# Four-tile attention visits in a fused retention and MLP kernel, with a new emission order

## The chip, the cores and the metric

The kernel runs on one core of one Trainium2 chip. The metric is the device time of one execution in microseconds; for the kernel before there are three runs. One more execution was taken by the hardware profiler. In its rows PE is TensorE (matmuls), PEld the weight loads that overlap it, DVE VectorE, ACT ScalarE, POOL GpSimd, SP SyncE. L701 is line 701 of the kernel's file.

## The reference

A causal retention layer without softmax, then an MLP with exact GELU:

```python
scores = scale * np.matmul(q, k.transpose(0, 1, 3, 2))      # q, k, v: (8, 8, 576, 64)
Dmat = np.where(rel >= 0, gamma[:, None, None] ** rel, 0.0) # rel = pos_i - pos_j, gamma by head
attn_out = np.matmul(scores * Dmat, v)
x = attn_out.transpose(0, 2, 1, 3).reshape(4608, 512)
h = x @ w_in                                                # (512, 2048)
g = 0.5 * h * (1.0 + erf(h / sqrt(2)))
out = g @ w_out                                             # (2048, 512)
```

## The kernel before

The retention runs in chunks of 128 positions (four of them and a tail of 64 per sequence). A unit is one chunk of one batch entry, all eight heads; after the first four units two batch entries form a pair (j = 0, 1) and are handled in one visit. For a chunk of a pair the tensor engine does four things:

- scores (`scores`, L535): keys times queries inside the chunk, 32 matmuls of 64x64 weights on 128 columns, into four PSUM banks `sc`. `masked` (L558, VectorE) multiplies them by the causal mask into `ret`.
- inner (`inner`, L600): scaled values `vh` times `ret`, eight matmuls per unit with weights of 128 rows and 64 columns, into one bank `o_ps` per unit.
- state (`state`, L619): keys times `vh`, 16 matmuls per pair with 128 rows and 64 columns, accumulated over chunks in one bank `u_ps`; `either` copies it to `u_sb` on VectorE or ScalarE, whichever the planner has free first.
- cross (`cross`, L653): the state up to the chunk before, times the queries, 16 matmuls of 64x64, added into the `o_ps` banks. `evacuate` (L672) scales them by `dqT` into `xT`, the input of the MLP.

A visit is emitted as inner of the pair that was scored earlier, its state, scores of the next pair, cross; sometimes scores stand alone. The tail chunk has its own forms (L525, L591). `scaled_v` makes `vh`, on VectorE in one instruction or on ScalarE in eight. The first groups are transposed on PE (L482), the later ones by DMA on SP's queue.

The MLP works on blocks of 512 tokens: `mlp1` (L701, `hT`) with GELU on ScalarE, `mlp2` (L746) for the first block, `part` (L885, `m`) with seven products of half blocks in place of eight for the others, `fast` (L966, `f`) in the same manner for the first product of the last blocks. Fillers (`warm`, L1180) run where the planner sees PE idle at the start.

Order is set at build time by a planner. It keeps a clock per engine (`T`), adds a duration for each piece (`pe`, `on`), follows which of the eight PSUM banks are held, and picks the next piece for PE. The string `ORDER` holds the order of loads on POOL's queue (k1, wi0, v5, ...) and numbers that shift the planner's choices by unit: s, b and z delay scores, inner and masks, p and u shift MLP pieces, and a names the units whose values ScalarE scales.

Of the kernel before, what the change touches and what calls it, by code (L numbers as in the profile page):

```python
# [9 lines left out]
FP32 = mybir.dt.float32  # L10
# [7 lines left out]
def kernel(  # L18
# [57 lines left out]
    AHEAD = 14  # L76
    A_TURNS = 2
    HOT = 5.3
    N_WARM = 10
    HOLD = 9  # L80

# [106 lines left out]
    def sum_w(i):  # L188
        w = w_out_sb[i]
        s = w_sum[i] = const.tile([128, 5, 256], BF16, name=f"w_sum{i}")  # L190
        b11, b12, b21, b22 = w[:, 0, 0:256], w[:, 0, 256:512], w[:, 1, 0:256], w[:, 1, 256:512]
        nc.vector.tensor_tensor(s[:, 0], b11, b22, op=ALU.add)
        nc.vector.tensor_tensor(s[:, 1], b12, b22, op=MINUS)
        nc.vector.tensor_tensor(s[:, 2], b21, b11, op=MINUS)
        nc.vector.tensor_tensor(s[:, 3:5], w[:, :, 0:256], w[:, :, 256:512], op=ALU.add)
        ws_at[i] = on("dve", 1.05, land_out[i]) + SEM

    SW_LATE, HW_LATE = 4.2, 2.8
    TURN_SHARES, STORE_SHARES = (0.455, 0.545), (0.455, 0.545)
# [125 lines left out]
    for x, keys in enumerate(zip(*HW_FIRST)):  # L325
        for n, (what, i) in enumerate(keys):
            land[what, i] = (4.6, 5.2)[n] + 0.75 * x
            t = tiles_of(i)
            cast_due[what, i] = (t[1] if what == "v" else t[0][:, "qk".index(what)], first[what, i])
    ORDER = ("wi1 k1 wi0 io q1 v0 q2 k2 v1 wi2 v2 k3 wi3 q3 v3 wi4 wi5 wi6 k4 q5 k5 q4 v5 wi7 wo1 wo0 k6 v4 dq2 "  # L330
# [7 lines left out]
             "b21+6.0").split()  # L338

    BY_ACT = {int(x[1:]) for x in ORDER if x[0] == "a"}  # L340
    S_LATE = {int(x[1:].split("+")[0]): float(x.split("+")[1]) for x in ORDER if x[0] == "s"}
# [106 lines left out]
    def u_of(bp, ci):  # L448
        return u_sb[2 if (bp, ci) == (1, 0) else ci % 2]
# [113 lines left out]
    def scaled_v(i):  # L563
        if len(later) > HP + 1:
            finish_later()
        ci = units[i][1]
        vh = vh_pool.tile([128, H, D], BF16, tag="vh", name="vh")
        at = land["v", i]
        by_act = i in BY_ACT
        if by_act:  # L570
            for h in range(H):
                nc.scalar.activation(vh[:, h, :], loaded[i][1][:, h, :], AF.Copy, scale=dv[:, h, ci:ci + 1])  # L572
            st[i]["V"] = on("act", 2.0, at) + SEM
        else:
            nc.vector.tensor_tensor(vh, loaded[i][1], dv[:, :, ci:ci + 1].to_broadcast([128, H, D]), op=ALU.mult)
            st[i]["V"] = on("dve", 0.685, at) + SEM
        st[i]["vh"] = vh
# [4 lines left out]
    def inner(i):  # L582
        bp, ci, j = units[i]
        s = st[i]
        pe_waits(max(s["R"], s["V"] if "vh" in s and i not in raw else land["v", i]))
        if j is None:
            s["o"] = [bank([128, HP, TAIL], FP32, "o_ps", False) for _ in range(2)]
            for h in range(H):
                for jj in range(2):
                    sl, e = slice(64 * jj, 64 * jj + 64), 64 * (h % 2)  # L590
                    nc.tensor.matmul(s["o"][jj][1][e:e + 64, h // 2, :], lhsT=s["vh"][sl, h, :], rhs=s["ret"][0][sl, h, :],  # L591
                                     start=(h < 2), stop=False, skip_group_check=True)
            s["B"] = pe(0.23, 2 * H, "quad")
        else:
            s["o"] = [bank([128, HP, 128], FP32, "o_ps")]
            o = s["o"][0][1]
            vals = loaded[i][1] if i in raw else s["vh"]
            for hp in range(HP):
                for e in range(2):
                    nc.tensor.matmul(o[64 * e:64 * e + 64, hp, :], lhsT=vals[:, 2 * hp + e, :], rhs=s["ret"][e][:, hp, :],  # L600
                                     start=(hp == 0), stop=(ci == 0 and hp == HP - 1), skip_group_check=True)
            s["B"] = pe(0.23, H, "col")
        s["Bdone"] = True
        if j is None:
            s_done.add(i)
        elif j == 1 and ci < NCI - 1 and (bp, ci) != (1, 0):
            u_due.append((bp, ci))

    def state(bp, ci):
        pair = pair_of[bp, ci]  # L610
        assert (bp, ci) == (1, 0) or nX > (pair_of[bp, ci - 1] if ci else pair_of[bp - 1, NCI - 2] if bp else [-1])[-1]
        if ci == 0:
            u_bank[bp] = bank([128, H, D], FP32, "u_ps")
        u_ps = u_bank[bp][1]
        pe_waits(state_at(bp, ci))
        for h in range(H):
            for j, i in enumerate(pair):
                keys = loaded[i][0][:, 1, h, :] if i < 4 else loaded[i][0][:, 1, h, j, :]
                nc.tensor.matmul(u_ps[64 * j:64 * j + 64, h, :], lhsT=keys, rhs=st[i]["vh"][:, h, :],  # L619
                                 start=(ci == 0 and h == 0), stop=(h == H - 1), skip_group_check=True)  # L620
        done = pe(0.26, 2 * H, "col")
        u_ready[bp, ci] = either(0.68, done, u_of(bp, ci), u_ps) + SEM
        u_due.remove((bp, ci))
        if ci == NCI - 2:
            release(u_bank[bp][0], u_ready[bp, ci])
        for i in pair:
            s_done.add(i)
        if pair[0] >= 4 and next_load[0] < len(groups):
            reload()
# [10 lines left out]
    def cross(n):  # L640
        g = groups[n]
        bp, ci, j0 = units[g[0]]
        if ci == 0:
            return
        u, qT = u_of(bp, ci - 1), sg[n]["qkT"]
        pe_waits(u_ready[bp, ci - 1])
        cols = slice(0, TAIL if j0 is None else C)
        for hp in range(HP):
            for e in range(2):
                for j in range(2):  # L650
                    o = st[g[0]]["o"][j][1] if j0 is None else st[g[j]]["o"][0][1]
                    sl = slice(64 * j, 64 * j + 64)
                    nc.tensor.matmul(o[64 * e:64 * e + 64, hp, :], lhsT=u[sl, 2 * hp + e, :], rhs=qT[sl, 0, 2 * hp + e, cols],  # L653
                                     start=False, stop=(hp == HP - 1), skip_group_check=True)
        done = pe(0.23, 2 * H, "quad")
        for i in g:
            st[i]["B"] = done

# [531 lines left out]
    while True:  # L1190
# [64 lines left out]
        if due:  # L1255
            _, kind, a = due[0]
            if kind == "X":
                cross(group_of[nX])
                for i in groups[group_of[nX]]:
                    evacuate(i)  # L1260
                    nX += 1
            elif kind == "U":
                state(*a)
            elif kind == "S":
                g, back = a
                for i in back:
# [81 lines left out]
```

## Time and profile before

| what | value |
|---|---|
| median of three runs | 285.37 us (285.2 to 285.39) |
| span of the profiled execution | 283.7 us |
| that execution's time outside the span | not given |
| PE busy | 278.0 us, 98%, 3361 matmuls |
| VectorE, ScalarE, GpSimd busy | 70%, 56%, 40% |
| granted TensorE clock | 0.998 |

The span runs from the program's first to its last instruction. A group's mean is the duration of one instruction; matmuls are pipelined, so the next one starts before the last has ended, and the pitch between starts is what a stream of them costs. A wait names who ended an engine's idle time.

### The profile page before, as it was taken

How to read it: one execution, taken by the hardware profiler on the slowest of the kernel's cores; microseconds unless marked ns; L12 is line 12 of the kernel's file. 1: busy time of each engine (PE TensorE's matmuls, PEld its weight loads, DVE VectorE, ACT ScalarE, POOL GpSimd, SP SyncE). 2: the span in 40 equal slices, each digit the busy share in tenths (PEclk: the TensorE clock that was granted, in tenths of full speed). 3: DMA queues.
4: the chain of work that ended last, by engine and by line, in shares of the span. 5: the costliest groups of instructions: out<-in, count | busy, mean ns of one | idle time of the engine just before them, and what ended most of it. 6: DMA issues, size and time to landing. Idle time of an engine off the chain costs nothing.

```text
span 283.7 us, 8075 instructions
## 1 busy us (share of the span) xinstructions
PE 278.0 (98%) x3361; PEld 207.6 (73%) x3361; DVE 199.7 (70%) x412; ACT 158.8 (56%) x362; POOL 114.0 (40%) x143
## 2 busy tenths in 40 slices
PE   8989999999999999999999999999999999999994
PEld 3577666688874588548855778558888888888894
DVE  5753483979865595898178867889669968966822
ACT  5676724755456635693298874564565374665320
POOL 8979987993364465625468552000000000000000
PEclk9999999999999999999999999999999999999999
DMA  9999999999999999999999999910003000400133
GB/s 150 165 182 173 188 180 163 146 142 147 172 161 195 190 147 128 156 229 149 135 197 203 147 137 150 222 21 2 0 2 128 23 2 0 151 0 2 74 114 111
DMA packets 152804, 35.39 MB, mean 125 GB/s; under 512 B 141120, under 2 KB 148928, under 8 KB 152768
## 3 DMA queue, kind: packets, MB, share of 16 engines
q0 software_dynamic: 116832, 18.10, 95.3%
q1 hardware_dynamic: 34528, 16.26, 32.9%
q10 hardware_dynamic: 1408, 0.52, 0.7%
q8 instruction: 26, 0.43, 0.7%
q14 instruction: 10, 0.08, 0.1%
HBM read 36.70 MB, written 9.44 MB: 163 GB/s over the span
## 4 chain that ended last, share of the span: by engine, by line
PE 92%; POOL 3%; DMA 3%; issue 0%; DVE 0%; POOLq 0%
PE m L885 35%; PE hT L701 29%; PE f L966 13%; PE oT L746 5%; PE o_ps L600 3%; PE sc L535 3%; DMA w_in<-in_moe_w_in_dram 3%; POOL qk L318 2%; PE o_ps L653 1%; PE u_ps L619 1%; PE qk_ps L482 1%; POOL v_ld L318 1%; POOL w_in L291 1%; PE sc L525 0%; PE o_ps L591 0%
## 5 line engine op out<-in xcount | busy, mean ns | idle before, releaser
L701 PE MATMUL hT<-xT,w_in 128*128 128x512 bf16 (+3 forms) x560 | 87.4, 312 | 0.8 <-DMA w_in<-in_moe_w_in_dram 0.8
L710 ACT ACTIVATE g<-hT 128x512 bf16<-128x512 f32 (+2 forms) x106 | 57.7, 556 | 36.9 <-PE hT L701 36.1
L701 PEld LDWEIGHTS <-w_in 128*128 128x128 bf16 x560 | 48.4, 98 | 33.8 <-DMA w_in<-in_moe_w_in_dram 1.0
L885 PEld LDWEIGHTS <-gs 128*128 128x128 bf16 x656 | 62.2, 98 | 7.7
L885 PE MATMUL m<-w_sum,gs 128*128 128x256 bf16 (+1 forms) x400 | 47.7, 268 | 0.0
L318 POOL DMA_DIRECT2D v_ld<-in_v_dram x40 | 34.0, 854 | 19.3 <-DMA qk_ld<-in_k_dram 8.8
L318 POOL DMA_DIRECT2D qk_ld<-in_k_dram x36 | 30.4, 851 | 21.7 <-DMA qk_ld<-in_q_dram 19.1
L558 DVE TENSOR_TENSOR ret<-sc,msk 128x512 bf16<-128x512 f32 x48 | 30.2, 683 | 12.2 <-PE sc L535 12.2
L318 POOL DMA_DIRECT2D qk_ld<-in_q_dram x36 | 30.4, 851 | 16.9 <-DMA qkT<-qk_ld 6.5
L885 PE MATMUL m<-w_out,gs 128*128 128x256 bf16 x256 | 32.5, 273 | 0.0
L885 PE MATMUL m<-w_sum,g 128*128 128x256 bf16 x256 | 30.9, 273 | 0.0
L572 ACT ACTIVATE vh<-v_ld,dv 128x64 bf16<-128x64 bf16 x120 | 30.0, 339 | 0.0
L782 DVE TENSOR_TENSOR gs<-g 128x1024 bf16<-128x1024 bf16 x32 | 21.8, 686 | 9.0 <-ACT g L710 8.2
L885 PEld LDWEIGHTS <-g 128*128 128x128 bf16 x256 | 24.9, 98 | 3.9
L991 ACT ACTIVATE g<-f 128x512 bf16<-128x512 f32 x36 | 20.2, 590 | 8.9 <-PE f L966 7.5
L786 DVE TENSOR_TENSOR gs<-g 128x1024 bf16<-128x1024 bf16 x32 | 21.6, 684 | 0.0
L672 DVE TENSOR_TENSOR xT<-o_ps,dqT 128x512 bf16<-128x512 f32 (+1 forms) x32 | 18.4, 617 | 4.5 <-PE o_ps L653 4.4
L966 PEld LDWEIGHTS <-w_in 128*128 128x128 bf16 x192 | 18.8, 98 | 2.2
L461 ACT CAST u_sb<-u_ps 128x512 bf16<-128x512 f32 x15 | 8.7, 587 | 16.0 <-PE u_ps L619 16.0
L461 ACT COPY o<-m 128x512 f32<-128x512 f32 x14 | 8.2, 587 | 15.7 <-PE m L885 15.7
L987 ACT ACTIVATE g<-p 128x512 bf16<-128x512 f32 x12 | 7.6, 630 | 14.1 <-DVE p L985 14.1
L966 PEld LDWEIGHTS <-wi 128*128 128x128 bf16 x144 | 14.0, 98 | 1.6
(96 smaller groups left out, 337.6 us busy)
## 6 DMA issues: line engine op xcount, KB each, us to landing
out_dram<-o SPq DMA_DIRECT2D x27, 256.0 KB, 6.3
v_ld<-in_v_dram POOLq DMA_DIRECT2D x32, 128.0 KB, 9.1
qk_ld<-in_k_dram POOLq DMA_DIRECT2D x28, 128.0 KB, 10.7
qk_ld<-in_q_dram POOLq DMA_DIRECT2D x28, 128.0 KB, 8.6
w_in<-in_moe_w_in_dram POOLq DMA_DIRECT2D x8, 256.0 KB, 7.3
w_out<-in_moe_w_out_dram POOLq DMA_DIRECT2D x8, 256.0 KB, 8.0
out_dram<-o SPq DMA_DIRECT2D x14, 128.0 KB, 2.1
qk_ld<-in_q_dram POOLq DMA_DIRECT2D x8, 64.0 KB, 11.4
```

The costliest lines, as they stand in the source:

```text
L318: nc.gpsimd.dma_start(dst, src[2 * bp + jj, :, ci * C:ci * C + n, :].rearrange("h s d -> s h d"))
L461: nc.scalar.copy(dst, src)
L558: nc.vector.tensor_tensor(r, t, by, op=ALU.mult)
L572: nc.scalar.activation(vh[:, h, :], loaded[i][1][:, h, :], AF.Copy, scale=dv[:, h, ci:ci + 1])
L672: nc.vector.tensor_tensor(x_of(i)[:, :, n * x:n * x + n], o, dqT[:, :, ci * C:ci * C + n], op=ALU.mult)
L701: nc.tensor.matmul(hT[:, m, :], lhsT=w[:, cc, o:o + 128], rhs=x_tiles[t][:, cc, lo:hi], start=(cc == 0), stop=(cc == N_DM - 1))
L710: nc.scalar.activation(g_of(t, m0 // 2)[:, m0 % 2:m0 % 2 + n, lo:hi], hT, AF.Gelu)
L782: nc.vector.tensor_tensor(s.rearrange("p m a b -> p m (a b)"), g[:, :, 0, :], g[:, :, 1, :], op=ALU.add)
L786: nc.vector.tensor_tensor(s, g[:, :, :, LEFT], g[:, :, :, RIGHT], op=MINUS)
L885: nc.tensor.matmul(m[:, 0 if apart else ts, :], lhsT=a, rhs=w[:, c0:c1], start=p in begins and mm == 0 and ts == 0, stop=mm == N_DF // 2 - ...
L966: nc.tensor.matmul(m[:, y, :], lhsT=a[:, c], rhs=d[:, c], start=p in (P1, P7) and y == 0 and c == 0, stop=c == 1, skip_group_check=True)
L991: nc.scalar.activation(g[:, :, rows, cols], m, AF.Gelu)
```

## The change

Output products and state are split along the contraction into halves of 64 rows. Where a pair's inner product, state, scores of the next pair and cross can all run together (`whole`), `visit` emits them as one piece on four 64x64 tiles of the array: three lists of matmuls per tile, woven by their columns. The first part holds inner from a unit's own row half, the state on the diagonal tiles (r == c), cross, and half of the scores on the other tiles. The middle part holds scores alone. The last part holds inner from the other row half, which writes the other unit's bank, the state on the other tiles and the rest of the scores. Ahead of the last part a nop on PE waits for the first matmul of the middle part. The masks, copies and evacuations of the visit follow the whole of it.

The planner's durations are set anew (`BOTH` is that of a visit), and `ORDER` is a new one: its loads are the same up to q4, and behind that loads and all shifts differ.

```diff
+    BOTH = 1.1
-        ws_at[i] = on("dve", 1.05, land_out[i]) + SEM
+        ws_at[i] = on("dve", 1.26, land_out[i]) + SEM
-    ORDER = ("wi1 k1 wi0 io q1 v0 q2 k2 v1 wi2 v2 k3 wi3 q3 v3 wi4 wi5 wi6 k4 q5 k5 q4 v5 wi7 wo1 wo0 k6 v4 dq2 "
-             "wo2 wo3 q7 wo4 k7 dq3 q11 b4+1.0 wo6 v8 wo5 q6 k8 wo7 v6 v7 k9 q10 q9 a28 k11 q8 v11 k10 q12 dq4 v9 "
...
+    ORDER = ("wi1 k1 wi0 io q1 v0 q2 k2 v1 wi2 v2 k3 wi3 q3 v3 wi4 wi5 wi6 k4 q5 k5 q4 wi7 wo0 dq2 v4 wo1 v5 wo2 "
+             "dq3 wo3 k8 wo4 wo7 q6 dq4 k7 wo6 wo5 q7 k6 q8 v6 q9 q11 v10 k9 v8 v7 q10 v12 v9 q12 k10 v11 k11 k12 "
...
-            st[i]["V"] = on("act", 2.0, at) + SEM
+            st[i]["V"] = on("act", 2.7, at) + SEM
-            s["B"] = pe(0.23, 2 * H, "quad")
+            s["B"] = pe(0.15, 2 * H, "quad")
+    HALF = [slice(0, 64), slice(64, 128)]
+
+    def weave(lists):
+        at, last = [0] * len(lists), None
+        while any(lists):
+            x = min((x for x in range(len(lists)) if lists[x]), key=lambda x: at[x])
+            cols, fn, a = lists[x].pop(0)
+            at[x] += cols
+            last = fn(*a)
+        return last
+
+    def whole(g, back):
+        if len(g) != 2 or len(back) != 2 or back[0] < 4 or units[back[0]][2] != 0:
+            return False
...
+        if ci and u_ready.get((bp, ci - 1), 1e9) > T["pe"] + 0.3:
+            return False
...
+        return max(max(st[i].get("V", 1e9), st[i]["R"]) for i in back) <= T["pe"] + 0.3
+
+    def visit(n, bp, ci):
...
+        for i in pair:
+            st[i]["o"] = [bank([128, HP, 128], FP32, "o_ps")]
+        got = [[bank([128, HP, 128], FP32, "sc") for _ in range(2)] for _ in g]
+
+        def inner_mm(j, r, e, hp, first):
+            s = st[pair[j]]
+            vals = loaded[pair[j]][1] if pair[j] in raw else s["vh"]
+            return nc.tensor.matmul(s["o"][0][1][HALF[e], hp, :], lhsT=vals[HALF[r], 2 * hp + e, :],
+                                    rhs=s["ret"][e][HALF[r], hp, :], start=first, stop=(not first and hp == HP - 1),
+                                    skip_group_check=True)
...
+        def state_mm(j, r, h):
+            return nc.tensor.matmul(u_ps[HALF[j], h, :], lhsT=loaded[pair[j]][0][HALF[r], 1, h, j, :],
+                                    rhs=st[pair[j]]["vh"][HALF[r], h, :], start=(ci == 0 and h == 0 and j == r), stop=(h == H - 1),
+                                    skip_group_check=True)
...
+        tiles = [(r, c) for r in range(2) for c in range(2)]
+        parts = [[[] for _ in tiles] for _ in range(3)]
+        for x, (r, c) in enumerate(tiles):
+            one, mid, two = (part[x] for part in parts)
+            one += [(128, inner_mm, (r, r, c, hp, hp == 0)) for hp in range(HP)]
+            two += [(128, inner_mm, (1 - r, r, c, hp, False)) for hp in range(HP)]
+            (one if r == c else two).extend((64, state_mm, (c, r, h)) for h in range(H))
+            if ci:
+                one += [(128, cross_mm, (r, c, hp)) for hp in range(HP)]
+            (two if r == c else one).extend((128, score_mm, (r, c, h)) for h in (range(4, 8) if r == c else range(4)))
+            mid += [(128, score_mm, (r, c, h)) for h in (range(4) if r == c else range(4, 8))]
+        weave(parts[0])
+        _, fn, a = parts[1][0].pop(0)
+        end = fn(*a)
+        weave(parts[1])
+        tc.add_manual_dep(nc.tensor.nop().ins, end.ins.name,
+                          mybir.DependencyInfo(mybir.DependencyClass.Sync, mybir.DependencyReason.DATA), reason="row tiles")
+        weave(parts[2])
+        done = pe(BOTH + (0.23 if ci else 0.0), 12 * H + 2 * H * (ci > 0), "quad")
...
+        u_ready[bp, ci] = either(0.68, done, u_of(bp, ci), u_ps) + SEM
...
+        masked(g[0])
+        for i in pair:
+            evacuate(i)
+        masked(g[1])
-        done = pe(0.26, 2 * H, "col")
+        done = pe(0.24, 2 * H, "col")
-        done = pe(0.23, 2 * H, "quad")
+        done = pe(0.2 if j0 is not None else 0.12, 2 * H, "quad")
                 g, back = a
+                if whole(g, back):
+                    visit(group_of[g[0]], *units[back[0]][:2])
+                    while u_due and state_at(*u_due[0]) <= T["pe"] + 0.3 * (nA >= 8):
+                        state(*u_due[0])
+                    continue
```

More of the change, by code (lines that the diff above doesn't have):

```diff
@@ L329 @@
             cast_due[what, i] = (t[1] if what == "v" else t[0][:, "qk".index(what)], first[what, i])
-    ORDER = ("wi1 k1 wi0 io q1 v0 q2 k2 v1 wi2 v2 k3 wi3 q3 v3 wi4 wi5 wi6 k4 q5 k5 q4 v5 wi7 wo1 wo0 k6 v4 dq2 "
[7 rows of a table removed]
-             "b21+6.0").split()
+    ORDER = ("wi1 k1 wi0 io q1 v0 q2 k2 v1 wi2 v2 k3 wi3 q3 v3 wi4 wi5 wi6 k4 q5 k5 q4 wi7 wo0 dq2 v4 wo1 v5 wo2 "
[7 rows of a table added]
+             "s0+1.0 u7+8 z29+8 p29+29 p24+28 s16+3 u4+28 b1+0.3 s1+0.6 u3+16 u2+8 p26+12").split()
     BY_ACT = {int(x[1:]) for x in ORDER if x[0] == "a"}
@@ L607, in inner @@
             u_due.append((bp, ci))
+    HALF = [slice(0, 64), slice(64, 128)]
[10 more added lines that the diff above has]
+            return False
+        bp, ci, _ = units[back[0]]
+        if (bp, ci) == (1, 0) or back != pair_of.get((bp, ci)) or nX != back[0]:
+            return False
+        if ci and u_ready.get((bp, ci - 1), 1e9) > T["pe"] + 0.3:
+            return False
+        if bp and ci == 1 and nX <= units.index((bp - 1, NCI - 1, None)):
+            return False
+        return max(max(st[i].get("V", 1e9), st[i]["R"]) for i in back) <= T["pe"] + 0.3
@@ new lines, in visit, with cross_mm, score_mm @@
+    def visit(n, bp, ci):
+        pair, g = pair_of[bp, ci], groups[n]
+        if ci == 0:
+            u_bank[bp] = bank([128, H, D], FP32, "u_ps")
+        u_ps, qkT = u_bank[bp][1], sg[n]["qkT"]
+        qT = sg[group_of[pair[0]]]["qkT"]
+        u = u_of(bp, ci - 1) if ci else None
+        at = max(st[i][x] for i in pair for x in "RV")
+        pe_waits(max(at, sg[n]["T"], u_ready[bp, ci - 1] if ci else 0.0))
+        for i in pair:
[7 more added lines that the diff above has]
+                                    skip_group_check=True)
+        def cross_mm(j, e, hp):
+            return nc.tensor.matmul(st[pair[j]]["o"][0][1][HALF[e], hp, :], lhsT=u[HALF[j], 2 * hp + e, :],
+                                    rhs=qT[HALF[j], 0, 2 * hp + e, :], start=False, stop=False, skip_group_check=True)
+        def state_mm(j, r, h):
+            return nc.tensor.matmul(u_ps[HALF[j], h, :], lhsT=loaded[pair[j]][0][HALF[r], 1, h, j, :],
+                                    rhs=st[pair[j]]["vh"][HALF[r], h, :], start=(ci == 0 and h == 0 and j == r), stop=(h == H - 1),
+                                    skip_group_check=True)
+        def score_mm(j, c, h):
+            return nc.tensor.matmul(got[j][h % 2][1][HALF[c], h // 2, :], lhsT=qkT[HALF[j], 1, h, HALF[c]],
+                                    rhs=qkT[HALF[j], 0, h, :], start=(h < 2), stop=True, skip_group_check=True)
+        tiles = [(r, c) for r in range(2) for c in range(2)]
[17 more added lines that the diff above has]
+        done = pe(BOTH + (0.23 if ci else 0.0), 12 * H + 2 * H * (ci > 0), "quad")
+        nonlocal nA, nB, nX
+        nA, nB, nX = nA + 2, nB + 2, nX + 2
+        for j, i in enumerate(g):
+            st[i]["sc"] = got[j], done
+        for i in pair:
+            st[i]["B"], st[i]["Bdone"] = done, True
+        u_ready[bp, ci] = either(0.68, done, u_of(bp, ci), u_ps) + SEM
+        if ci == NCI - 2:
+            release(u_bank[bp][0], u_ready[bp, ci])
+        for i in pair:
+            s_done.add(i)
+        if next_load[0] < len(groups):
+            reload()
+        masked(g[0])
+        for i in pair:
+            evacuate(i)
+        masked(g[1])
```

12 rows, old and new, of the table ORDER are left out of this document.

## The prediction

> **What bounds the kernel now.** I read the page first, then the waits of the tensor engine, then its busy time by stretch, then its timeline around the attention visits.
>
> ```profile
> span 283.7 us, 8075 instructions
> PE 278.0 (98%) x3361; PEld 207.6 (73%) x3361; DVE 199.7 (70%) x412; ACT 158.8 (56%) x362; POOL 114.0 (40%) x143
> PE 92%; POOL 3%; DMA 3%; issue 0%; DVE 0%; POOLq 0%
> ```
>
> The chain that ended last is 92% PE; VectorE and ScalarE have room on average. Who made PE wait, and its busy time in two stretches:
>
> ```profile
> PE warm L1187 <- DVE zeros L118: 1.2, 1, 1.2
> PE hT L701 <- DMA w_in<-in_moe_w_in_dram: 0.8, 1, 0.8
> ```
>
> (us in total, times, longest.) Start and end of a stretch, its length, then busy us and matmul count of PE, weight loads, VectorE, ScalarE and GpSimd, the granted clock, DMA share and GB/s:
>
> ```profile
> 18.60:60.00 41.40, 41.40 (x527) 28.51 (x526) 23.67 (x62) 23.54 (x55) 37.08 (x46) 1.00 2.10 169
> 60.00:194.00 134.00, 134.00 (x1790) 93.07 (x1789) 101.36 (x197) 80.89 (x199) 60.46 (x73) 1.00 1.76 157
> ```
>
> The reader is to see that PE waited twice in all, both times early, and that from 18.6 us to 194 us it is busy in every microsecond at a granted clock of 1.00. After the second wait the time is therefore a sum of matmul pitches and of the losses where the array changes its tile shape. An edit pays only if it shortens that sum or leaves less of it behind the wait. The wait:
>
> ```profile
> 12.89 0.61 PE L701 MATMUL hT<-xT,w_in 128*128 128x128 bf16 x8
> 13.33 1.03 PE L1180 MATMUL warm<-zeros 128*128 128x512 bf16 x4
> ...
> 17.07 0.62 PE L701 MATMUL hT<-xT,w_in 128*128 128x128 bf16 x8
> 18.47 1.05 PE L701 MATMUL hT<-xT,w_in 128*128 128x256 bf16 x8 [0.78 <-DMA w_in<-in_moe_w_in_dram]
> ```
>
> PE has nothing else to do until a w_in tile lands, and resumes at 18.47. A 128-column hT matmul costs 0.44/8 = 0.056 us.
>
> **The change part by part.** Times are from start to next start, since matmuls overlap. One visit of before, whole:
>
> ```profile
> 149.59 1.03 PE L701 MATMUL hT<-xT,w_in 128*128 128x512 bf16 x4
> 150.55 0.64 PE L600 MATMUL o_ps<-ret,vh 128*64 128x128 bf16 x16
> 151.02 0.42 PE L619 MATMUL u_ps<-vh,qk_ld 128*64 128x64 bf16 x16
> 151.37 0.64 PE L535 MATMUL sc<-qkT 64*64 64x128 bf16 x32
> 151.84 0.39 PE L653 MATMUL o_ps<-qkT,u_sb 64*64 64x128 bf16 x16
> 152.16 0.61 PE L701 MATMUL hT<-xT,w_in 128*128 128x512 bf16 x2
> ```
>
> Rounds. The 32 scores run on four 64x64 tiles: eight rounds in 0.47, 0.056 a round plus some 0.02 once after a change of shape. The 16 inner products (two 128x64 tiles) take 0.47 too, eight rounds. Cross takes 0.32: four rounds of 0.056 are 0.22, so leaving the small tiles costs about 0.10. State takes 0.35 up to the first score; eight rounds of 64 columns at about 0.032 are 0.26, so the change from 128x64 to 64x64 costs 0.09, and with the restart 0.02 it is some 0.12 a change.
>
> What a whole visit does with them. It splits inner and state along the contraction, so 32 + 32 matmuls replace 16 + 16, each on a tile of half the rows. Four tiles now carry what two carried: still eight rounds of 0.056 and eight of 0.032 a tile. The streamed time stays at 0.45 + 0.26 + 0.45 + 0.22 = 1.38 us, with or without the change. The gain is only the shape change inside the visit: -0.12.
>
> What it adds. Between its first and last third a nop on PE waits for the first score of the middle third; the last third writes the output banks from the other row half. Behind the nop stands all of PE's queue, and nothing else waits there. How long a score takes to end, and what a wait instruction takes in PE's queue:
>
> ```profile
> L535 PE MATMUL sc<-qkT x448: 213/216/240, 32.2 to 190.7; 64*64 64x128 bf16 x150
> L535 PEldq EVENT_SEMAPHORE  x10: 51/51/51, 73.6 to 189.8; - x10
> ```
>
> The awaited score ends 0.216 to 0.240 after its start, and the middle third's four rounds take 0.224. So the wait costs 0 to 0.02 of its own, up to 0.05 of hand-over (the wait instruction, the nearest row), and a restart of 0.02. The tiles on the diagonal do their state rounds in the first third (0.70 against 0.67 for the others), the others in the last: 0.03 lost at the cut. I take 0.05 + 0.02 + 0.03 = 0.10. From below it is 0, if tiles run past one another and the wait is over in time. From above it is 0.20: a drain like a shape change (0.12) with hand-over and imbalance (0.08). A visit is then -0.12 + 0.10 = -0.02 us, with ends -0.12 and +0.08. In the order of the built programs six of the 14 score sets of paired units become whole visits, two of them without cross: 6 x -0.02 = -0.12 (-0.7 to +0.5).
>
> That tiles pass one another can be seen in the trace: the program has all scores of the tail (L525, two tiles) ahead of cross (L653, four tiles).
>
> ```profile
> 158.26 0.38 PE L525 MATMUL sc<-qkT 64*64 64x64 bf16 x12
> 158.45 0.24 PE L653 MATMUL o_ps<-qkT,u_sb 64*64 64x128 bf16 x2
> 158.47 0.23 PE L525 MATMUL sc<-qkT 64*64 64x64 bf16 x4
> 158.53 0.40 PE L653 MATMUL o_ps<-qkT,u_sb 64*64 64x128 bf16 x14
> ```
>
> Two cross matmuls start at 158.45 on idle tiles, before the last four scores. So the order within a third costs little, and I add nothing for it.
>
> Shape changes elsewhere. Counted in the two programs behind the w_in wait there are 67 before and 62 after. Six go with the six visits, so the new order adds one: +0.12 (0 to +0.24).
>
> The new order, early. The first 21 loads on POOL's queue are the same, so the w_in tile of the wait lands when it did. Ahead of it the changed program has 56 hT matmuls of 128 columns instead of 48 and 21 fillers (warm) instead of 23; all other PE work there is equal in number. PE resumes at the same 18.47 with eight matmuls less to do: 8 x 0.056 = -0.45. If that load lands 0.45 later, nothing is left of it.
>
> Loads and transposes. On POOL v5 moves behind wi7, wo0 and wo1, and later w_out tiles, q and k change places; SP gets one store between other transposes. PE waited for no load after 18.5 us, so this costs nothing unless a load becomes later than its slack, which the page does not show.
>
> Scaling V. Eight tiles move from ScalarE to VectorE (15 to 7 named in the order).
>
> ```profile
> L572 ACT ACTIVATE vh<-v_ld,dv 128x64 bf16<-128x64 bf16 x120 | 30.0, 339 | 0.0
> L575 DVE TENSOR_TENSOR vh<-v_ld,dv 128x512 bf16<-128x512 bf16 x21 | 14.3, 700 | 0.0
> ```
>
> ScalarE loses 8 x 2.0 = 16 us, VectorE gains 8 x 0.68 = 5.4 us, to 205 us of the span. The cover is VectorE's 30% of idle time; gone, it would show as masks arriving late (rival 3). The planner's durations (pe and on calls) issue nothing themselves.
>
> Sum: -0.12 + 0.12 - 0.45 = -0.45 us, so a span of 283.3 for 283.7. The profiled execution's own full time is not given; the median run, 285.37, lies 1.7 above its span, and I carry that over: 284.9.
>
> **The rivals.** 1. The cut costs nothing. Then each visit saves the full 0.12: -0.72 + 0.12 - 0.45 = -1.05, 284.3. For it: tiles do pass one another (158.45). Against: the nop holds the whole queue, and a score ends no sooner than 0.216.
>
> 2. Only the fillers change. If the early matmuls meet another early wait, or the load lands later, -0.45 is gone: 285.4, no change. For it: the stretch has many small waits on VectorE filled by warm matmuls. Against: the loads' order is the same up to there.
>
> 3. Banks come back too late (slower). A visit holds seven of the eight banks to its very end, and only then do the masks start; before, they started while cross still ran:
>
> ```profile
> 152.00 1.29 DVE L558 TENSOR_TENSOR ret<-sc,msk 128x512 bf16<-128x512 f32 x2
> 153.20 1.28 DVE L672 TENSOR_TENSOR xT<-o_ps,dqT 128x512 bf16<-128x512 f32 x2
> ```
>
> Cross ran to 152.16. PE can fill one bank after the visit: the change of shape and four hT matmuls, about 0.10 + 0.87 = 0.97 after the last small matmul's start. The first bank is back after 0.22 (its end) + 0.65 = 0.87. The margin is 0.1 us. It decides as soon as VectorE is over 0.1 us late at a visit's end, for example inside one of its sums or in a copy of the state. If it is late by 0.3 on average, 6 x (0.3 - 0.1) = +1.2, 286.1. For it: more VectorE work, and it was busy 101 of 134 us where the visits lie. Against: a bank freed by ScalarE just before helps.
>
> 4. Row tiles cannot share the state's bank. In a visit the two row halves write u_ps, one bank, at the same time on different partitions; no row of before does that. If they took turns, the state's eight rounds would double in the first and in the last third: 2 x 0.26 = 0.51 a visit, +3.1 in all, 288.0 with the other terms. The Trainium skill, page TensorEngine Tiling (Array Packing), section Gotcha 1: PSUM Pressure, says that different row tiles cannot access the same PSUM bank simultaneously. By that rule this rival holds; no run here shows it yet. Against it, worked from the program alone: each half writes other partitions, so no address is shared.
>
> **How the numbers follow.** Forecast 0.45, rival 1 0.20, rival 2 0.13, rival 3 0.16, rival 4 0.06. What a measurement of this kernel can tell from no change is about 0.2%, 0.57 us: faster means below 284.80, slower above 285.94. The forecast's own ends (visit costs) put 0.18 of its 0.45 below 284.80 and 0.27 within; with rival 1 faster is 0.38, with rival 2 same is 0.40, slower (3 and 4) 0.22. The range 284.0 to 286.2 takes in rivals 1 to 3 at their prices and leaves out rival 4, the late end of rival 3 and the far end of rival 1, 0.17 in all.
>
> **What would show it.** Right: PE waits once for w_in, for about 0.45 us less, and resumes near 18.47; a whole visit with cross lasts about 1.6 us from its first inner product to the next hT, with a gap of 0.05 to 0.1 in its middle; PE's idle time after 18.5 stays zero. Wrong: visits of 1.5 us (rival 1) or over 2 us (rival 4); rows of hT or m matmuls waiting for VectorE behind a visit (rival 3); resumption well after 18.47, or a new early wait (rival 2); a wait of PE for a transposed q/k tile, which I have not priced.

## The result: no gain, 0.5% longer

The changed kernel takes 287.27 us in the median of 20 runs (285.89 to 289.29); the kernel before, run beside it, 285.48 (285.19 to 287.94). The ratio is 1.0054, 95% interval 1.0035 to 1.0072. The forecast was 284.9, range 284.0 to 286.2. In the experiments below one execution each of wide_visits, early_k10 and early_no_visits showed a lower granted clock (0.988 to 0.994) and took 4 to 5 us longer than the median; medians, ranges and ratios of these three are given without it, while the 285.94 and 286.92 that an expectation names count it in.

The page of the profiled execution, the shortest of the 20 (285.89), whose span is only 0.4 us above that of before: span, busy times, the instruction queue, the chain that ended last.

```profile
span 284.1 us, 8405 instructions
...
PE 278.0 (98%) x3559; PEld 207.7 (73%) x3559; DVE 204.2 (72%) x421; ACT 144.5 (51%) x298; POOL 113.8 (40%) x143
...
q8 instruction: 28, 0.46, 0.7%
...
PE 98%; issue 1%; DVE 0%
```

By the page nothing but PE bounds it. VectorE and ScalarE moved about as forecast (+4.5, -14.3 us). The waits of PE, us in total, times, longest:

```profile
PE u_ps L658 <- issue: 1.4, 1, 1.4
PE warm L1281 <- DVE zeros L119: 1.2, 1, 1.2
```

The wait for w_in is gone; in its place stands one gap that no semaphore ends ("issue"). PE's timeline around two whole visits, the third and the fifth of six:

```profile
143.84 0.42 PE L649 MATMUL o_ps<-ret,vh 64*64 64x128 bf16 x16
...
144.54 0.42 PE L663 MATMUL sc<-qkT 64*64 64x128 bf16 x16
144.84 0.42 PE L649 MATMUL o_ps<-ret,vh 64*64 64x128 bf16 x16
...
145.44 0.39 PE L795 MATMUL hT<-xT,w_in 128*128 128x512 bf16 x1
...
181.55 0.42 PE L649 MATMUL o_ps<-ret,vh 64*64 64x128 bf16 x16
...
182.98 0.22 PE L663 MATMUL sc<-qkT 64*64 64x128 bf16 x1
184.58 0.22 PE L658 MATMUL u_ps<-vh,qk_ld 64*64 64x64 bf16 x2 [1.39 <-issue]
...
184.76 0.39 PE L795 MATMUL hT<-xT,w_in 128*128 128x512 bf16 x1
```

The third visit lasts 145.44 - 143.84 = 1.60 us, its middle four rounds 0.30 for 0.22 of streaming. The fifth has the same work and lasts 3.21: it stops five matmuls from its end. PE's instructions come by DMA in packets of 16 KB on queue q8, 28 for 3559 matmuls (26 for 3361 before), one for some 127 with their weight loads. (The Trainium skill, page Trainium Architecture — The Big Picture, section The software stack, gives 64 bytes an instruction, by estimate 128 such pairs in 16 KB; the trace agrees with its 127.) The DMA queues ahead of the gap and across it, as packets, MB and share, first in 174.8 to 181.9 us, then the instruction row of 181.9 to 183.4:

```profile
q0 software_dynamic: 3003, 0.37, 98.3%
q1 hardware_dynamic: 1347, 0.79, 77.9%
q14 instruction: 1, 0.01, 1.7%
...
q8 instruction: 1, 0.02, 5.3%
```

For 7 us of full queues no packet came for PE; the next ran from 182.0 to 183.3, by which time PE stood still; PE goes on 1.3 us after its end. That suggests theory F (feed): the visits use up instructions faster than these come in behind the loads. Its rivals: V, the form of the visits costs the time itself; O, the new order does; L, a part of O that the first runs brought up: the loads, and so the tiles transposed by DMA, come later.

### The profile page after: what moved, and what is told of

Its sections match the earlier page's. It is cut to its first block, busy times and chain, and to the rows that moved or that the text cites. A ratio compares the mean times of both kernels' runs of the same rounds, so it can differ in the third digit from the quotient of the medians.

```text
span 284.1 us, 8405 instructions
## 1 busy us (share of the span) xinstructions
PE 278.0 (98%) x3559; PEld 207.7 (73%) x3559; DVE 204.2 (72%) x421; ACT 144.5 (51%) x298; POOL 113.8 (40%) x143
## 4 chain that ended last, share of the span: by engine, by line
PE 98%; issue 1%; DVE 0%
PE m L979 35%; PE hT L795 30%; PE f L1060 13%; PE oT L840 5%; PE o_ps L601 2%; PE warm L1274 2%; PE qk_ps L483 2%; PE warm L1281 2%; PE sc L536 2%; PE o_ps L649 1%; PE o_ps L747 1%; PE sc L663 1%; PE u_ps L713 1%; PE u_ps L658 1%; PE sc L526 0%
## 5 line engine op out<-in xcount | busy, mean ns | idle before, releaser
L804 ACT ACTIVATE g<-hT 128x512 bf16<-128x512 f32 (+2 forms) x107 | 58.3, 554 | 42.1 <-PE hT L795 41.5
L576 DVE TENSOR_TENSOR vh<-v_ld,dv 128x512 bf16<-128x512 bf16 x29 | 19.0, 683 | 0.0
L462 ACT COPY o<-m 128x512 f32<-128x512 f32 x13 | 7.6, 586 | 19.6 <-PE m L979 19.6
L840 PE MATMUL oT<-w_out,g 128*128 128x512 bf16 x64 | 15.0, 379 | 0.0
```

The lines of the kernel that those rows point to most:

```text
L804: nc.scalar.activation(g_of(t, m0 // 2)[:, m0 % 2:m0 % 2 + n, lo:hi], hT, AF.Gelu)
L840: nc.tensor.matmul(oT, lhsT=g_of(t, m // 2)[:, m % 2, cols], rhs=w_out_sb[m // 2][:, m % 2, :], start=(m == 0), stop=(m == N_DF - 1))
```

## The experiments

Times are medians of ten to twelve executions (six of no_visits, five of early_no_visits, four of fine_before); "ratio" is to the kernel before, run on the same chip in the same session, with its 95% interval. Medians of different sessions are compared only roughly: the kernel before was at 285.5 to 286.05 in them. A visit is called narrow in the form of the change (64 rows) and wide on 128 rows.

**again**: the changed kernel, unaltered.

> The changed kernel once more, nothing altered. Theory F (feed): the six whole visits issue matmuls so fast that TensorE's next piece of instructions (16 KB, about 129 matmuls with their weight loads) is still on its way behind the loads; the first profile has one gap of 1.39 us inside a visit that no semaphore ends. So the time is again 286 to 289, varying by over 1 us between executions, and the profile shows one to four gaps of 0.3 to 2 us put down to issue after 90 us, in or just behind visits, not necessarily the same ones. Theory V (visits): the visits' own form costs the time, the nop and the narrow matmuls; then every visit is equally long, 1.7 us or more, and the gap of 1.39 us need not return. Theory O (order): the new order of loads and tiles costs it; then waits for DMA or VectorE show on TensorE.

Measured 287.24 (285.94 to 289.26), ratio 1.0062 (1.0038 to 1.0086). Its waits:

```profile
PE sc L663 <- DMA qkT<-qk_ld: 1.2, 2, 0.7
PE o_ps L601 <- issue: 0.3, 1, 0.3
PE u_ps L658 <- issue: 0.2, 1, 0.2
```

The row of L601 (at 14.46 us) is no such gap: a filler's record is missing there, and the pieces around it start 0.65 us apart in after as well. The gap in the fifth visit is back, but smaller (the visit lasts 2.04 us, and the 0.2 in its row is less than the 0.3 that theory F expected at the least), and there are waits for transposed tiles in the second (118 us) and the sixth (190 us). The kernel loses time in more than one place, and not in the same ones each time. Undisturbed visits are again 1.60.

**no_visits**

```diff
     def whole(g, back):
+        return False
```

> The changed kernel with whole() answering no: its order, its early part and its planner durations stay, every visit runs as before, with 191 fewer matmuls. Theory F: no stall is left, and the early gain remains; 284.7 to 285.5. Theory V: the same, 284.7 to 285.5, so this run does not tell F from V. Theory O: it stays near 287, with waits of TensorE for DMA or VectorE.

287.50, ratio 1.0068 (1.0042 to 1.0094). Its profile waits 2.2 us for transposed tiles (at 68 and 162 us) and 0.6 us for VectorE, with no visit left. So the order has a fault of its own. F and V alone expected 284.7 to 285.5 and are out as only cause. (The planner places later pieces differently without visits; the kernel is no clean half of the change.)

**wide_visits**

```diff
-        weave(parts[0])
...
-        weave(parts[2])
+        for i in pair:
+            vals = loaded[i][1] if i in raw else st[i]["vh"]
+            for hp in range(HP):
+                for e in range(2):
+                    nc.tensor.matmul(st[i]["o"][0][1][HALF[e], hp, :], lhsT=vals[:, 2 * hp + e, :], rhs=st[i]["ret"][e][:, hp, :],
...
```

Behind the inner products on all 128 rows follow state, scores and cross as in the kernel before.

> The changed kernel, every engine's order as it is, but inside a whole visit the inner products and the state run on all 128 rows (16 + 16 matmuls for 32 + 32), without the nop and the weaving; 192 matmuls fewer in all. Each visit loses its cut (0.12) and gets its shape change back (0.12). Theory F: with 80 matmuls instead of 112 in a visit most of the stalls go; 284.7 to 286. Theory V: also about 285, but then no gap is seen in any profile of the narrow visits. Theory O: 287, as the order of everything else is untouched.

285.77 (284.69 to 287.2), ratio 1.0002 (0.9983 to 1.0021): 1.5 us below again, inside the range of F and V, while O alone expected 287. So neither the order nor the visits cost all of it. The wide visits last 1.61 (1.39 without cross) for 1.60 (1.37) of the narrow ones, and the fifth is not disturbed.

**light_after**

```diff
+    LEFT_OUT = 18
...
+        if i not in loaded and i >= LEFT_OUT:
+            loaded[i] = loaded[LEFT_OUT - 2]
...
-            nc.gpsimd.dma_start(dst, src[2 * bp + jj, :, ci * C:ci * C + n, :].rearrange("h s d -> s h d"))
+            if i < LEFT_OUT:
+                nc.gpsimd.dma_start(dst, src[2 * bp + jj, :, ci * C:ci * C + n, :].rearrange("h s d -> s h d"))
```

> The changed kernel with the loads of q, k and v of units 18 to 35 left out (these units compute on the tiles of units 16 and 17); TensorE, VectorE, ScalarE and SP issue the same instructions in the same order, and TensorE waited for none of these loads. About half of the DMA time in 100 to 180 us goes. Theory F: the pieces of instructions come in time, the visits have no gap, and the time is 284.0 to 285.0, with less than 0.5 us between executions. Theories V and O (as far as O is not DMA): it stays near 287.

284.91 (284.34 to 285.49), ratio 0.9973 (0.9961 to 0.9984): without these loads the changed kernel is the shorter one, by 0.3%. (Units 18 to 35 are computed on the tiles of units 16 and 17, so the kernel leaves out their results.) Its executions still differ by 1.15 us, where under 0.5 was expected. The stretch 100 to 182 us of after, then of this kernel (last columns: clock, DMA share, GB/s), and its waits:

```profile
100.00:182.00 82.00, 82.00 (x1161) 56.29 (x1162) 61.60 (x125) 41.39 (x87) 40.32 (x49) 1.00 2.03 161
```

```profile
100.00:182.00 82.00, 81.63 (x1123) 56.61 (x1128) 61.59 (x124) 40.93 (x86) 0.00 (x0) 1.00 0.42 83
...
PE warm L1285 <- DVE zeros L120: 1.2, 1, 1.2
PE qk_ps L487 <- DMA qk<-in_q_dram: 0.9, 1, 0.9
PE o_ps L605 <- issue: 0.3, 1, 0.3
```

With the DMA share down from 2.03 to 0.42 all narrow visits are whole, the fifth 1.59. (L605 is again a missing filler's record.) V is out: the form is the same. F and L are not told apart here, since both live on the loads.

**early_k10.** Why are the loads late? POOL's timeline, of before and then of after: the load of k10, and that of q15, which takes the buffer of unit 10's q and k and so waits for their transposes:

```profile
48.68 1.38 POOL L318 DMA_DIRECT2D qk_ld<-in_k_dram  x2 [0.29 <-issue]
...
61.05 1.75 POOL L318 DMA_DIRECT2D qk_ld<-in_q_dram  x2 [0.22 <-issue]
```

```profile
52.28 1.40 POOL L319 DMA_DIRECT2D qk_ld<-in_k_dram  x2
...
64.93 1.76 POOL L319 DMA_DIRECT2D qk_ld<-in_q_dram  x2 [3.37 <-DMA qkT<-qk_ld]
```

In the new ORDER k10 stands 3.6 us later, the first transposes of SP with it, and everything behind q15 starts 3.9 us later (5.9 in again).

```diff
-            load(what, n)
+            load(what, n, issue=(what, n) != ("k", 10))
+            if (what, n) == ("q", 10):
+                load("k", 10, planned=False)
```

> The changed kernel with one load moved on POOL's queue: k10 (unit 10, the first short group, whose tiles SP transposes first) is issued right behind q10, some 3.6 us sooner, where it stands about that early in the kernel before; every other engine issues the same instructions in the same order. Theory L (late loads): in the profiles of the changed kernel the load of q15 waits 3.4 to 5.5 us for the two transposes of unit 10, before the change 0.2 us; everything behind it lands 4 to 7 us later and the transposed tiles reach TensorE with 0 to 1 us to spare. So the wait on POOL shrinks by about 3 us, TensorE waits for no qkT, and the time is 284.6 to 286.0. Theory F (feed alone): the instruction gaps in the visits remain and the time stays at 286 to 289. Theory V (the visits' form): 287.

286.67 (285.73 to 289.31), ratio 1.0044 (1.0014 to 1.0075): above the range of L, inside that of F alone. POOL's wait is gone, PE's isn't:

```profile
62.98 1.75 POOL L320 DMA_DIRECT2D qk_ld<-in_q_dram  x2 [0.38 <-DMA qk_ld<-in_k_dram]
...
PE sc L668 <- DMA qkT<-qk_ld: 0.9, 1, 0.9
```

The wait is at 119 us, for units 20 and 21. Before the change their transposed tiles landed at 117.7 and their scores began at 119.5, 1.8 us to spare. Now they land at 119.3, while the visit begins at 118.1 (before 118.7) and has scores in its first part. k10 alone is not the whole of L. The fifth visit loses 0.32 us here, for 1.6 in after: a PE that is late at 119 us is less early for the packet at 182. Here the two waits stand in for each other, so undoing one half returns little.

**early_no_visits**, the same move in no_visits:

> The same move of k10, and every visit as before (whole() answers no; 191 matmuls fewer). Without the move this kernel took 287.5 and waited 2.2 us for transposed tiles. Theory L: 284.9 to 285.7, no wait for qkT. Theory F predicts the same 284.9 to 285.7 only if the loads play no part in the 287.5, which it can't explain. If another part of the new order costs the time, it stays at 287.

289.53 (286.22 to 290.38), ratio 1.0102 (1.0054 to 1.0150). A miss for all three expectations. What this order lacks besides k10 stays open.

**early_wide**, the same move in wide_visits:

> The same move of k10 with the whole visits on 128 rows (80 matmuls a visit, no nop). Theory L: 284.6 to 285.5, with none of the long executions of wide_visits (to 290.6). The difference to early_k10 is then what the narrow form of the visits costs or brings: by the cut and the shape change alone 0 +/- 0.3 us, with late instructions (theory F) early_k10 is longer by 0.3 to 1.5 us and shows gaps put down to issue.

285.72, ratio 0.9991 (0.9971 to 1.0011), 0.95 below early_k10, and 0.2 above the range of L. Six of the twelve executions took 284.9 to 285.4, six 286.1 to 286.7. The profiled one is of the upper six and shows their difference:

```profile
PE sc L664 <- DMA qkT<-qk_ld: 1.6, 1, 1.6
```

**late_k10**, the kernel before with k10 issued behind v10:

> The kernel before the change with the opposite move: k10 is issued behind v10, some 4 us later, nothing else altered. Theory L: the load of q15 waits 3 to 5 us for the transposes of unit 10 where it waited 0.2, the transposed tiles come with 0 to 2 us to spare, and the time rises by 0.5 to 2 us, to 286 to 287.5, with more spread. Theories F and V: 285.5, unchanged.

286.31, ratio 1.0019 (0.9998 to 1.0041), with a wait of 0.7 us for unit 10's own transposed tiles at 67 us. The time is at the low end of L's price, but the interval just takes in no change. The load of q15 did wait, 6.4 us, and starts at 67.98 for 61.05; yet units 20 and 21 have their tiles 2.2 us ahead of need, for 1.8 without the move. So a late k10 makes its own tile late; that the loads behind it make a later tile late is not shown by this run.

**light_wide**, **light_before**: the loads left out of wide_visits and of the kernel before.

> wide_visits (whole visits on 128 rows) with the loads of q, k and v of units 18 to 35 left out, as in the second light kernel. With all loads the narrow visits cost 1.2 to 1.3 us more than the wide ones (287.24 to 285.94; 286.92 to 285.72), though an undisturbed narrow visit is as short as a wide one in the profiles (1.60 to 1.61, 1.37 to 1.39 us). Theory F (instructions late behind the loads): without the loads the difference goes; this kernel takes 284.7 to 285.2, within 0.3 of the narrow one's 284.91. Theory V (the narrow form itself): the difference stays, this kernel takes 283.6 to 283.9.

> The kernel before the change with the same loads left out. It waited for no load after 18.5 us, so by theory L (loads and transposed tiles late) little changes: 285.2 to 285.5, with less spread. Then the changed kernel without these loads is 0.3 to 0.6 us shorter than this one, about what was forecast (0.45), and all that it loses beyond is due to the loads. If this one falls to 284.9 too, the early part gains nothing and the forecast's largest term was wrong.

light_wide 284.87, ratio 0.9973 (0.9957 to 0.9990); light_before 285.16, ratio 0.9978 (0.9965 to 0.9991). Narrow and wide now differ by 0.04 us, where they differed by 1.5: the narrow form costs time only beside the loads. Against light_before the changed kernel gains 0.25 us (two sessions), a little under the 0.3 to 0.6 expected. The kernel before, too, is 0.4 us shorter without these loads.

**fine_before**, **light_fine**: the feed without any visit.

```diff
-                nc.tensor.matmul(hT[:, m, :], lhsT=w[:, cc, o:o + 128], rhs=x_tiles[t][:, cc, lo:hi],
-                                 start=(cc == 0), stop=(cc == N_DM - 1))
+                for c0 in range(lo, hi, 128 if t == 3 else hi - lo):
+                    c1 = c0 + 128 if t == 3 else hi
+                    nc.tensor.matmul(hT[:, m, c0 - lo:c1 - lo], lhsT=w[:, cc, o:o + 128], rhs=x_tiles[t][:, cc, c0:c1],
+                                     start=(cc == 0), stop=(cc == N_DM - 1), skip_group_check=True)
```

> The kernel before the change, with the 64 hT matmuls of 512 columns of its fourth block (142.7 to 159.9 us) cut into 256 of 128 columns: 192 matmuls more, about as many as the change adds, and nothing else altered. By the pitches 64 x (4 x 0.056 - 0.216) = +0.5 us. Theory F: the pieces of 129 matmuls are used up in 7 us and arrive late; one to three gaps put down to issue between 143 and 170 us, 0.3 to 2 us each, and the time is 286.5 to 289. If instructions always come in time: 286.0, no such gap.

> The same cut of the hT matmuls with the loads of units 18 to 35 left out. Theory F: with the DMA engines freer the pieces come in time or nearly so; 0.5 us above the uncut kernel without these loads, 285.7 to 286.0, and gaps under 0.3 us in all. If a piece's arrival does not depend on the loads, the gaps are those of the kernel with all loads.

(The kernel leaves out the right sums of that block; its instructions are what is timed. The block runs at 114 to 131 us, not at the place that the expectation names.) fine_before 288.46 (four executions), ratio 1.0084 (1.0056 to 1.0112); light_fine 286.21, ratio 1.0015 (1.0001 to 1.0029). Timeline and waits of fine_before:

```profile
114.39 5.52 PE L703 MATMUL hT<-xT,w_in 128*128 128x128 bf16 x96
119.85 0.64 PE L600 MATMUL o_ps<-ret,v_ld 128*64 128x128 bf16 x16
120.32 0.42 PE L619 MATMUL u_ps<-vh,qk_ld 128*64 128x64 bf16 x16
120.67 0.57 PE L535 MATMUL sc<-qkT 64*64 64x128 bf16 x25
121.65 0.30 PE L535 MATMUL sc<-qkT 64*64 64x128 bf16 x7 [0.41 <-issue]
...
PE sc L535 <- DMA qkT<-qk_ld: 0.8, 1, 0.8
PE sc L535 <- issue: 0.4, 1, 0.4
```

After 96 narrow hT matmuls and 57 more PE stops in the middle of an old visit, waiting for no semaphore, and goes on 1.43 us after the end of the packet that ran from 119.2 to 120.2. light_fine, the same instructions beside fewer loads, has no such gap: there the same packet, the twelfth, ended 4.5 us before this matmul. It takes 1.05 us more than light_before; 0.6 of that are the pitches (256 in 14.39 us for 64 x 0.216), 0.4 are not accounted for. So the gap of F is shown without a visit. Its price is not: fine_before is 2.9 us above the kernel before, of which 0.6 are pitches and 0.4 the gap, and the wait of 0.8 is at 111.5 us, ahead of the cut block, so the cut has not caused it.

**moved_wide, moved_narrow, moved_before.** Three more loads change places: v17 behind k19, v18 and v19 behind k21, which brings the q and k of units 18 to 21 forward.

```diff
+    MOVED = {('k', 10): ('q', 10), ('v', 17): ('k', 19), ('v', 18): ('k', 21), ('v', 19): ('k', 21)}
```

> early_wide with three more loads moved on POOL's queue, all other engines as they were: v17 is issued behind k19, v18 and v19 behind k21. The q and k of units 18 to 21 so go two places ahead, some 3 us, and the v tiles, needed 9 us or more after they land, behind. Theory L: six of the twelve executions of early_wide were 284.9 to 285.4, the others 286.1 to 286.7, one profiled with a wait of 1.6 us at 119 us; without that wait nearly all fall in the lower group, median 284.9 to 285.3, faster than the kernel before by 0.2 to 0.6. If the wait comes from the new order's other parts (stores, DMA as a whole), the two groups stay.

> The same four moves with the changed kernel's narrow visits. Theories L and F together: no wait at 119 us, but TensorE so arrives at the visit at 182 us without delay and meets its late piece of instructions: a gap of 0.3 to 1.6 us put down to issue in that visit, median 285.6 to 286.6, 0.5 to 1.3 over the wide one. Theory L alone: as the wide one, 284.9 to 285.3.

> The kernel before the change with the loads of v17, v18 and v19 moved in the same way. Its profile shows no wait for transposed tiles, but 6 of its first 20 executions took 286.5 to 287.9 against 285.2 to 285.6 for most. Theory L: the median stays at 285.3 to 285.5, with fewer long executions. If it gains more than 0.3 in the median, the loads held it too.

moved_wide 284.97, ratio 0.9973 (0.9958 to 0.9989), eleven of twelve executions at 284.8 to 285.6: the version that beats both kernels, the one before by 0.3%. moved_before 285.39, ratio 0.9980 (0.9968 to 0.9992), its longest execution 285.84; it is 0.33 below the kernel before in that session, so the order of the loads held that kernel a little, too. moved_narrow 286.95, ratio 1.0038 (1.0016 to 1.0061), longer than the 285.6 to 286.6 that L and F together expected. The waits of moved_wide, then of moved_narrow:

```profile
PE warm L1269 <- DVE zeros L120: 1.2, 1, 1.2
PE hT L783 <- DMA w_in<-in_moe_w_in_dram: 0.7, 1, 0.7
PE qk_ps L489 <- DVE qk L463: 0.6, 1, 0.6
```

```profile
PE sc L669 <- DMA qkT<-qk_ld: 1.0, 1, 1.0
```

In moved_wide the tiles of units 20 and 21 land 4.5 us ahead of need, and PE waits for nothing after 20 us. In moved_narrow the wait at 119 us is gone too, but the fifth visit lasts 1.95, and the sixth waits 1.0 us for a transposed tile that was issued at 180.0 and landed at 190.9 (in moved_wide it was issued at 182.8 and landed at 187.0).

**fifth_wide, fifth_narrow, last_two_wide**: where the 2.0 us between those two lie.

```diff
+        visits.append(1)
+        if len(visits) != 5:
...
+        else:
...
```

Behind `else` stands the code of wide_visits. fifth_narrow has `== 5` there, last_two_wide `< 5`.

> moved_narrow with the fifth whole visit (182 us) alone on 128 rows, 32 matmuls fewer. Theory F: the late piece of instructions is met in this visit, because the fourth and fifth use up 208 matmuls between 172 and 184 us; with it wide the gap of 0.3 to 1.6 us there goes or shrinks below 0.3, and the time is 285.0 to 286.2. If the cost is spread over all narrow visits, or lies in the wait at 190 us, little changes: 286.4 to 287.

> moved_wide with the fifth whole visit alone narrow, 32 matmuls more. Theory F: a piece that comes late hits it here too, though the fourth visit now uses up 32 fewer: 285.1 to 286.0, a gap of 0 to 1 us in that visit. If the cost is spread over all six, a sixth of 2.0: 285.3, no gap.

> moved_narrow with the fifth and the sixth visit wide, the first four narrow. If the whole cost lies in the last two visits: 284.9 to 285.3, as moved_wide. If the tiles transposed late at 190 us come from the narrow visits before, by way of later loads, the wait there stays: 285.6 to 286.5 with waits for qkT. If the cost is spread evenly, four sixths of it: 286.3.

fifth_wide 285.63, ratio 0.9984 (0.9961 to 1.0007); fifth_narrow 285.10, ratio 0.9978 (0.9958 to 0.9997); last_two_wide 285.37, ratio 0.9985 (0.9964 to 1.0006). Widening one of six visits takes back 1.3 of the 2.0 us, by the medians of two sessions, widening the sixth as well 0.3 more. The profile of fifth_wide waits after the fillers once, at the start:

```profile
PE qk_ps L489 <- DMA qk<-in_q_dram: 0.3, 1, 0.3
```

that of last_two_wide once, at 74 us, far ahead of its wide visits:

```profile
PE sc L542 <- DMA qkT<-qk_ld: 0.7, 1, 0.7
```

And fifth_narrow, whose fifth visit has the very same 112 matmuls but 128 fewer ahead of it, lasts 1.60 there, without a gap. As far as the gap goes, it isn't the visit that costs; it is which visit meets the end of a packet while the next is behind the loads. The four profiles with all six visits narrow beside the full loads have the gap in the fifth (3.21, 2.04, 1.92 and 1.95 us); it is in none of the others.

It is also at the same place, between the 107th and the 108th of the visit's 112 matmuls. PE's timeline there in again, early_k10 and moved_narrow:

```profile
184.11 0.22 PE L663 MATMUL sc<-qkT 64*64 64x128 bf16 x1
184.55 0.22 PE L658 MATMUL u_ps<-vh,qk_ld 64*64 64x64 bf16 x2 [0.23 <-issue]
...
184.28 0.22 PE L668 MATMUL sc<-qkT 64*64 64x128 bf16 x1
184.61 0.22 PE L663 MATMUL u_ps<-vh,qk_ld 64*64 64x64 bf16 x2
...
183.35 0.22 PE L669 MATMUL sc<-qkT 64*64 64x128 bf16 x1
183.71 0.22 PE L664 MATMUL u_ps<-vh,qk_ld 64*64 64x64 bf16 x2
```

| kernel | 19th packet on q8, us | 107th starts | 108th starts | behind the packet's end |
|---|---|---|---|---|
| after | 182.02 to 183.29 | 182.98 | 184.58 | 1.29 |
| again | 181.72 to 182.97 | 184.11 | 184.55 | 1.58 |
| early_k10 | 181.84 to 183.13 | 184.28 | 184.61 | 1.48 |
| moved_narrow | 180.89 to 182.36 | 183.35 | 183.71 | 1.35 |
| light_after | 176.98 to 178.07 | 183.95 | 183.96 | 5.89 |

In all four PE goes on 1.3 to 1.6 us after the end of the same packet, whenever it got there; in light_after, where the packet had ended 5.9 us ahead, it does not stop. In fifth_wide the matmul of the same number, the 2519th, comes at 188.9, 6.4 us behind the packet's end. What fills the 1.3 to 1.6 us the traces do not show. The size of the gap depends on both times: early_k10 and again reach the place over 1 us later than after and so lose less, and moved_narrow loses little because its packet ended 0.9 us sooner.

## Point by point

- **The visit** (-0.12 + 0.10 = -0.02 us): right. Undisturbed, 1.60 for 1.61, and 1.37 for 1.39 without cross. The middle part is 0.08 longer than its streaming, inside the forecast 0.05 to 0.1. Rival 1 (a cut that costs nothing) is out. A nop-less visit wasn't tried.
- **Four row tiles in the state's bank** (rival 4): refuted. Both row halves wrote u_ps in the same rounds at full pace; a turn-taking visit would have lasted 2.1. The Trainium skill, page TensorEngine Tiling (Array Packing), Gotcha 1: PSUM Pressure, says that different row tiles cannot access the same PSUM bank simultaneously; here, on separate partitions, the measurement differs from it and decides.
- **Banks back too late** (rival 3): no row of after waits for VectorE behind a visit. The change came out slower, but by none of the mechanisms given for it.
- **Early, -0.45**: partly right. In the profile of after the w_in wait is gone; in others up to 1.3 us wait there or for the first q and k. Where no later wait interferes the gain of the whole change is 0.25 (light_before to light_after) to 0.42 (moved_before to moved_wide).
- **Loads and transposes, nothing**: the first step that failed. The prediction called it free "unless a load becomes later than its slack" and did not work out the slack, though the trace of before holds it: landing of each pair's transposed tiles against the start of its scores, 1.8 us at the least, against a k10 that moved by 3.6 us and scores that a whole visit wants at its beginning. Moving k10 back was not enough (early_k10); with the q and k of units 18 to 21 ahead of v as well (moved_wide against wide_visits) 0.8 us and the spread are back. The last sign of being wrong that the prediction names, a wait for a transposed tile, is the one that came.
- **What no step named**: the supply of PE's instructions. The change adds 198 matmuls, 192 of them in six visits of 1.4 to 1.6 us, while the load queues are full. It was priced at nothing because PE's time behind the w_in wait was taken for a sum of pitches and shape changes; that step failed, too. Seen in the traces it cost 1.61 us once (after) and 0.32 to 0.44 in three others. Beside the full loads narrow is 1.0 to 2.0 us longer than wide, and widening one visit returns 1.3; how much of that is the gap and how much the late tile at 190 us is not told apart.
- **Shape changes elsewhere** (+0.12): not measured apart.
- **The sum**: without both faults (light_after, light_wide, moved_wide) the time is 284.9 to 285.0, where the forecast stood, with either form of the visit. That is in part luck: without the loads the kernel before is shorter, too, and the gain is 0.25 where 0.45 was forecast. From moved_wide (284.97) to again (287.24) it is 2.3 us. By way of wide_visits the loads cost 0.8 of it and the narrow form 1.5, by way of moved_narrow 0.3 and 2.0: the two overlap, and the split is only roughly known. Two of the narrow profiles also wait at 190 us for a transposed tile; what makes it land late stays open.

## What to carry to other kernels

Where one engine is busy throughout, list for each transfer when it lands and when it is first used before calling a new order of loads free. Count instructions as well as cycles: a stretch of many short matmuls beside full DMA queues can run out of instructions, and the profile shows it only as a gap put down to "issue", or, where it is as short as 0.3 us, in the timeline alone. Before blaming the new form of the work, run it with the loads taken out.

## Not expected of the hardware

- PE's instructions arrive in 16 KB packets, one for some 127 matmuls and weight loads, and share the DMA engines with the loads: gaps of 0.3 to 1.6 us in a visit, always before the same matmul and 1.3 to 1.6 us past the end of the same packet; none with the DMA share at 0.42.
- Two halves of the array's rows wrote one PSUM bank on separate partitions without loss (visits of 1.60 and 1.37 us).
- Two waits behind one another are not added: a PE that was 1.1 us late at 119 us lost 0.3 on its instructions at 184 (early_k10), one that was not lost 1.6 (after). A sooner packet does the same: moved_narrow was not late at 119 us and lost 0.35.
